# Attention and a gated MLP on one core: GpSimd's broadcasts of reciprocals go ahead of its copies of P, and one copy of P moves to ScalarE

## The chip, the cores and the metric

One core of a Trainium2 chip runs the kernel. The metric is the device time of one execution in microseconds (us). The core's engines are TensorE (PE in the profile; PEld is its weight load), VectorE (DVE), ScalarE (ACT), GpSimd (POOL) and SyncE (SP, which here only issues DMAs).

## The reference

Causal attention by blocks of 64 over batch 8, 8 heads, 576 positions and head size 64, then a gated MLP over all 4608 tokens:

```python
scores = scale * np.matmul(q, k.transpose(0, 1, 3, 2))
scores = np.where(block_i >= block_j, scores, -1e9)
attn = np.exp(scores - scores.max(-1, keepdims=True))
attn = attn / (attn.sum(-1, keepdims=True) + 1e-9)
x = np.matmul(attn, v)                    # (8, 8, 576, 64) -> (4608, 512)
gate = 1 / (1 + np.exp(-(x @ w_gate)))    # w_gate, w_val: 512 x 1536
out = (gate * (x @ w_val)) @ w_out        # w_out: 1536 x 512
```

## The kernel before

The work is done on pairs of heads: 32 pairs, four to a batch. A script written out by hand (FRONT) runs the first pairs, up to some 125 us. Then one step of a loop over p runs for each pair until some 460 us, and in the same stretch TensorE multiplies the first third of the MLP's hidden units (L179, L188) for the batches that are done; those matmuls are dealt between the attention's at a set rate, about 36 of them in a step. After that the rest of the MLP runs with TensorE busy throughout (L1341, L1411).

In a step, the table REST sets the order in which parts are issued, and so how each engine's queue stands, for the pair p and the two ahead of it. Three pairs are in work at once:

- **"AV"** and **"fin"** of pair p-2: TensorE multiplies the turned probabilities in the tile G by V (L358, `bank<-G,VS`, 44 matmuls), and VectorE multiplies the result by the broadcast reciprocals `rb` (L703, `xT<-bank,rb`), which also frees the PSUM bank pair that AV wrote. There are three such bank pairs. The scores of pair p take two of them right behind AV and need the third, AV's own, for their last block. ScalarE then makes the high part of xT (L831) and GpSimd the low part (L844, "xl").
- **"s"**, **"t"** of pair p: scores on TensorE (L358, with KH, KL, QH, QL), maxima on VectorE (L487, L541), eight exps on ScalarE (L499) and a ninth for the last 64 positions (L543), all into a buffer Z or XB by turns.
- **"tr3"**, **"tr2"**, **"trm"** of pair p: VectorE turns the exps in place by 32x32 blocks (L598, three instructions; the last, of 1408 columns, waits for L543). Behind it come the sums plus 1e-9 (L565), the reciprocal (L566) and a turned copy `rT` (L568), and GpSimd's queue writes rT to DRAM (`r_d<-rT`).
- **"mv"** and **"mc"** of pair p-1: the turned blocks are moved between groups of 32 partitions into G, in 16 quarters of 32x800. Nine go by DMA (L621, four from GpSimd's queue and five from SyncE's), three are copied by ScalarE (L624) and four by GpSimd (L615, `move_pool`). G has one buffer, so this starts when AV of the pair ahead is done.
- **"rb"** of pair p-1: three DMAs from GpSimd's queue (L292, `rb<-r_d`) read the reciprocals from DRAM and broadcast them over 64 partitions each.
- **"k"**, **"ql"**, **"q"**: K and Q of pair p+1 are turned (L390) and split in high and low parts: KH on ScalarE (L395), KL on GpSimd (L405), QL on VectorE (L409).

Everything on one engine is executed in its queue's order. ScalarE's third copy, of quarter (2, 2), stands behind the exp of the sixth score block by a line in `move`; the first two come when AV has freed G. `hL` (L218) is the low part of the MLP's hidden values: on GpSimd, or on VectorE for the last of a batch's four.

Of the kernel before, what the change touches and what calls it, by code (L numbers as in the profile page):

```python
# [21 lines left out]
AHEAD = 3  # L22
KEEP = 11

REST = (("AV", 0), ("fin", 0), ("s", 3), ("mv", 0), ("xl", 0), ("mc", 0), ("rb", 0), ("t", 4), ("tr3", 1), ("tr2", 1), ("k", 0), ("trm", 0), ("ql", 0), ("q", 0), ("trl", 1), ("trt", 2))
NB = 25
B_OF = {2: (0, 3), 3: (6, 4), 0: (14, 1), 1: (16, 2)}
LT = 14
# [45 lines left out]
def attn_glu_kernel(ctx: ExitStack, tc: tile.TileContext, q, k, v, w_gate, w_val, w_out, out):  # L74
# [26 lines left out]
    def behind(ins, other):  # L101

        tc.add_manual_dep(ins, other.name, mybir.DependencyInfo(mybir.DependencyClass.NoSync,
                                                                mybir.DependencyReason.DATA), reason="order")
# [123 lines left out]
    with ExitStack() as s2:  # L228
# [105 lines left out]
        maxima, exps = [], []  # L334
# [3 lines left out]
        def mark(engine, ins):  # L338
            last[engine] = ins.ins

        def chain(engine, ins):
            if not scripted and engine in last:
                behind(ins.ins, last[engine])
            mark(engine, ins)
# [83 lines left out]
        def attend(p):  # L428
# [179 lines left out]
            def quarter(k):  # L608
                c, a = k if isinstance(k, tuple) else quarters[k]
                return dict(out=Gc[32 * c:32 * c + 32, a], in_=Zc[32 * a:32 * a + 32, c])  # L610

            def move_pool():

                for k in (8, 10, 11, (3, 3)):
                    chain("POOL", nc.gpsimd.tensor_copy(**quarter(k)))  # L615

            def move():

                for k in range(12):
                    if k not in (8, 10, 11):  # L620
                        ins = (nc.sync if k % 2 else nc.gpsimd).dma_start(**quarter(k))  # L621
                        (mark if k % 2 else chain)("moves" if k % 2 else "POOL", ins)
                for i in range(3):
                    ins = nc.scalar.copy(**quarter((i, i)))  # L624
                    if i > 1:
                        behind(ins.ins, exps[-3])
                    mark("ACT", ins)

            def tr_main(i):
# [219 lines left out]
            def step(what, is_fine=False, alt=False, queue=nc.sync):  # L849
# [4 lines left out]
                elif what[0] == "s":  # L854
                    s_blocks({"s3": (3,), "s2": (2,), "sl": (1, 0)}[what])
                elif what == "t":
                    s_tail()
                elif what == "rb":
                    if moved:
                        recip(2, nc.gpsimd)  # L860
                elif what == "trm":
                    if moved:
                        turned()
                    else:
                        recip()
                elif what == "mv":
                    if moved:
                        move()
                elif what == "mc":
                    if moved:  # L870
                        move_pool()
                elif what == "xl":
                    lower_x()
                elif what in ("tr3", "tr2"):
                    tr_main(int(what[2]))
                elif what == "trl":
                    tr_low()
                elif what == "trt":
                    tr_tail()
                elif what == "fin":  # L880
                    finish()
                else:
                    av()
# [388 lines left out]
        for p in range(N_FIRST + 1, n + 1):  # L1272
# [5 lines left out]
            tick = 0  # L1278
            for what, places in REST:
                if what == "AV" and far:  # L1280
# [24 lines left out]
                for _ in range(places if now else 6 if what == "tr3" else 0):  # L1305
                    pe_ticks.append(pe_last[0])
                    acc += rate
                    while acc >= 1:
                        acc -= 1
                        left -= 1  # L1310
                        ins = next(mlp, None)
# [256 lines left out]
```

## Time and profile before

| what | value |
|---|---|
| median of 3 runs | 1099.28 us (1096.95 to 1099.8) |
| the profiled execution | 1099.69 us |
| its span, first to last instruction | 1097.8 us |
| TensorE busy | 1080.7 us (98%) |
| VectorE busy | 862.1 us (79%) |
| ScalarE busy | 602.7 us (55%) |
| GpSimd busy | 532.3 us (48%) |
| granted TensorE clock | 1.000 of 2.4 GHz |

The span is what the profiler saw of the core; the execution's time is 1.89 us longer. Busy shares are means over stages that differ: the engines other than TensorE are full in the stage of the loop and half idle in the MLP that follows.

### The profile page before, as it was taken

The numbers are of one execution on the slowest core, as the hardware profiler recorded it, in microseconds if no ns is written. First come the engines' busy times: TensorE is split into PE (matmuls) and PEld (weight loads), VectorE is DVE, ScalarE is ACT, GpSimd is POOL, SyncE is SP. The second block draws the span as 40 slices with busy tenths as digits, with TensorE's granted clock in tenths as the row PEclk, the third lists the DMA queues.
The fourth block names the chain that finished last, engine by engine and source line by source line (L and its number), as shares of the span: only waits on it lengthen the run. The fifth ranks groups of instructions, "written<-read, shape, count | busy, mean of one in ns | idle before, by whom it ended". The sixth has DMA issues, their size and how long they took to land.

```text
span 1097.8 us, 19466 instructions
## 1 busy us (share of the span) xinstructions
PE 1080.7 (98%) x6593; PEld 929.5 (85%) x6593; DVE 862.1 (79%) x1488; ACT 602.7 (55%) x1321; POOL 532.3 (48%) x692
## 2 busy tenths in 40 slices
PE   8899999999999999999999999999999999999998
PEld 6577777778787778778899999999999999999997
DVE  6899999898989898787699768578785585665744
ACT  6887777777787777643353444534454142341421
POOL 3655499898989898710113030321305336243340
PEclk9999999999999999999999999999999999999999
DMA  8797599899888887745033362350886517345251
GB/s 162 162 206 159 128 184 190 187 189 197 185 194 177 200 175 184 198 122 170 22 97 103 123 221 78 144 187 34 293 296 230 188 50 224 103 128 186 74 164 58
DMA packets 264619, 174.87 MB, mean 159 GB/s; under 512 B 200988, under 2 KB 222092, under 8 KB 263880
## 3 DMA queue, kind: packets, MB, share of 16 engines
q1 hardware_dynamic: 247000, 148.54, 50.6%
q0 software_dynamic: 7008, 17.68, 6.9%
q10 hardware_dynamic: 10512, 7.41, 2.3%
q8 instruction: 52, 0.85, 0.3%
q14 instruction: 47, 0.39, 0.1%
HBM read 104.73 MB, written 47.60 MB: 139 GB/s over the span
## 4 chain that ended last, share of the span: by engine, by line
PE 83%; DVE 4%; DMA 4%; ACT 3%; POOL 2%; issue 2%; SPq 1%; ACTq 0%; DVEq 0%; POOLq 0%
PE b L1341 32%; PE m L1411 12%; PE bank L358 11%; PE m L179 10%; PE m L188 7%; PE b L1411 7%; PE bank L179 3%; SPq L292 1%; DMA rqk<-in_q_dram 1%; DMA rqk<-in_k_dram 1%; DMA rb<-r_d 1%; PE bank L188 1%; POOL G L615 1%; PE bank L363 1%; ACT XB L499 1%
## 5 line engine op out<-in xcount | busy, mean ns | idle before, releaser
L1341 PE MATMUL b<-XH,w 128*128 128x384 f32 x1344 | 349.0, 335 | 0.0
L1341 PEld LDWEIGHTS b<-XH,w 128*128 128x128 f32 x1344 | 243.8, 188 | 3.6
L1341 PE MATMUL b<-XL,w 128*128 128x384 f32 x672 | 223.5, 335 | 0.0
L1136 POOL TENSOR_TENSOR XB<-XB 128x384 f32<-128x384 f32 x20 | 21.5, 1076 | 238.0 <-DMA XB<-xT_d 238.0
L1341 PEld LDWEIGHTS b<-XL,w 128*128 128x128 f32 x672 | 126.1, 188 | 1.7
L1411 PE MATMUL m<-wo,hH 128*128 128x512 f32 x368 | 119.9, 391 | 0.0
L358 PE MATMUL bank<-G,VS 128*64 128x64 f32 (+3 forms) x1264 | 95.0, 305 | 2.6 <-POOL G L615 1.5
L358 PEld LDWEIGHTS bank<-G,VS 128*64 128x64 f32 x1264 | 64.6, 137 | 35.1 <-issue 7.6
L1364 ACT ACTIVATE g<-g 128x384 f32<-128x384 f32 x72 | 37.8, 525 | 93.1 <-DVE g L1377 49.3
L1149 ACT CAST XH<-XB 128x1536 fp32r<-128x1536 f32 (+2 forms) x72 | 65.1, 941 | 35.7 <-DVE XB L1147 27.3
L188 PE MATMUL m<-wo,hH 128*128 128x512 f32 x256 | 83.8, 393 | 0.0
L179 PE MATMUL m<-XH,wg 128*128 128x512 f32 x240 | 81.2, 394 | 0.4 <-ACT t L203 0.4
L179 PE MATMUL m<-XH,wv 128*128 128x512 f32 x240 | 81.2, 395 | 0.0
L1411 PEld LDWEIGHTS m<-wo,hH 128*128 128x128 f32 x368 | 69.0, 188 | 12.9
L487 DVE TENSOR_REDUCE nm<-bank 128x2 f32<-128x1024 f32 (+1 forms) x96 | 76.9, 801 | 2.2 <-ACT Z L499 0.6
L1150 DVE TENSOR_TENSOR XL<-XB,XH 128x1536 fp32r<-128x1536 f32 (+2 forms) x72 | 75.8, 1085 | 0.0
L1411 PE MATMUL m<-wo,hL 128*128 128x512 f32 x184 | 72.1, 392 | 0.0
L1411 PE MATMUL b<-wo,hH 128*128 128x512 f32 (+1 forms) x216 | 71.4, 383 | 0.0
L1405 POOL TENSOR_TENSOR pr<-pr,pr 128x512 f32<-128x512 f32 x33 | 42.6, 1296 | 42.6 <-DMA pr<-part_d 29.6
L499 ACT ACTIVATE Z<-bank,nm 128x512 f32<-128x512 f32 (+3 forms) x104 | 53.5, 529 | 7.8 <-DVE nm L487 4.5
L188 PEld LDWEIGHTS m<-wo,hH 128*128 128x128 f32 x256 | 47.9, 188 | 9.9 <-issue 0.2
L1349 POOL TENSOR_TENSOR hL<-v,hH 128x384 fp32r<-128x384 f32 x36 | 38.9, 1094 | 33.0 <-ACT hH L1348 30.3
(219 smaller groups left out, 2626.3 us busy)
## 6 DMA issues: line engine op xcount, KB each, us to landing
pr<-part_d SPq DMA_DIRECT2D x66, 256.0 KB
XB<-xT_d SPq DMA_DIRECT2D x16, 576.0 KB
part_d<-pr SPq DMA_DIRECT2D x36, 256.0 KB
rqk<-in_q_dram SPq DMA_DIRECT2D x120, 72.0 KB
rqk<-in_k_dram SPq DMA_DIRECT2D x120, 72.0 KB
out_dram<-pr SPq DMA_DIRECT2D x33, 256.0 KB
wgv_d<-st SPq DMA_DIRECT2D x8, 896.0 KB
w<-wgv_d SPq DMA_DIRECT2D x4, 1792.0 KB
```

What stands on the lines that cost most here:

```text
L179: mm = nc.tensor.matmul(ps, lhsT=lh, rhs=rh, start=(i == 0), stop=(i == n - 1))
L188: mm = nc.tensor.matmul(ps, lhsT=lh[:, f, t * P:(t + 1) * P], rhs=rh, start=(f == i == 0), stop=(f == F1 - 1 and i == 2))
L358: pe_last[:] = [pin("PE", nc.tensor.matmul(*args, **kw)).ins]
L487: mark("DVE", nc.vector.tensor_reduce(out=nm_()[:, c0:c0 + 2], in_=ps[:, :, c:c + n], axis=AX.X, op=ALU.max, negate=True))
L499: mark("ACT", nc.scalar.activation(out=dst, in_=src, func=AF.Exp, bias=nm_()[:, c0 + h:c0 + h + 1], accum_out=sm[:, 5 * h + i:5 * h + i + 1]))
L1149: nc.scalar.copy(out=XO[j][0][:, a:b], in_=x)
L1150: sub = nc.vector.tensor_sub(out=XO[j][1][:, a:b], in0=x, in1=XO[j][0][:, a:b].bitcast(F32))
L1341: mm = nc.tensor.matmul(ps, lhsT=lh, rhs=rh, start=(first and k == 0), stop=(k == n - 1), skip_group_check=not first)
L1349: (nc.vector if q else nc.gpsimd).tensor_sub(out=hL[:, f, n:n + N2], in0=h, in1=hH[:, f, n:n + N2].bitcast(F32))
L1364: mark2("ACT", nc.scalar.activation(out=t, in_=c, func=AF.Tanh, scale=0.5))
L1405: nc.gpsimd.tensor_add(out=pr[t], in0=pr[t], in1=other)
L1411: mm = nc.tensor.matmul(po[t][:, cols], lhsT=lh[:, f, t * P:(t + 1) * P], rhs=wo[:, f, e, cols], start=((whole or half == 0) and i == 0), ...
```

## The change

In REST, "rb" stands ahead of "mc", so GpSimd issues the three broadcasts ahead of its copies. GpSimd copies three quarters, not four, and ScalarE copies the fourth, quarter (3, 3), behind the exp of the eighth score block.

```diff
-REST = (... ("mv", 0), ("xl", 0), ("mc", 0), ("rb", 0), ("t", 4), ...)
+REST = (... ("mv", 0), ("xl", 0), ("rb", 0), ("mc", 0), ("t", 4), ...)
...
             def move_pool():
 
-                for k in (8, 10, 11, (3, 3)):
+                for k in (8, 10, 11):
                     chain("POOL", nc.gpsimd.tensor_copy(**quarter(k)))
...
-                for i in range(3):
+                for i in range(4):
                     ins = nc.scalar.copy(**quarter((i, i)))
                     if i > 1:
-                        behind(ins.ins, exps[-3])
+                        behind(ins.ins, exps[-3 if i == 2 else -1])
                     mark("ACT", ins)
```

GpSimd's queue in one step of the loop (L621 are its four moves, L844 the low part of xT, L218 and L402 belong to the MLP and to the next pair's Q):

```order
 L621 DMA G<-XB 32x800 x4
 L844 TENSOR_TENSOR XL_435<-xT,XH_434 128x576
-L615 COPY G<-XB 32x800 x4
-L292 DMA rb<-r_d 64x576
-L292 DMA rb<-r_d 64x64
-L292 DMA rb<-r_d 64x512
+L292 DMA rb<-r_d 64x576
+L292 DMA rb<-r_d 64x64
+L292 DMA rb<-r_d 64x512
+L615 COPY G<-XB 32x800 x3
 L218 TENSOR_TENSOR hL<-h_1925,hH 128x512
 L402 TENSOR_SCALAR KQ<-KQ 128x128
```

The three broadcasts have moved ahead of the copies, and one copy is gone.

ScalarE's queue in the same step (the exps of one pair, the last two of the eight and the ninth):

```order
 L214 CAST hH<-h_1925 128x512
 L499 ACTIVATE Z,sm_108<-bank,nm 128x4x32 x2
+L624 COPY G<-XB 32x800
 L543 ACTIVATE Z,sm_108<-bank,nm 128x4x160
 L203 ACTIVATE t<-m 128x512
```

The new copy stands between the eighth exp and the ninth. It stands there in every step of the loop that has the moves, 22 of 23; in the last one four copies follow each other.

VectorE's queue once, near the end of the loop (L703 is xT of the last pair but one, L1062 to L1140 prepare weights and sums for the second part of the MLP):

```order
 L1062 TENSOR_SCALAR raw<-cT 128x512
+L1064 SCALAR_TENSOR_TENSOR raw<-raw 128x512
+L1065 TENSOR_TENSOR cT<-cT,raw 128x512
 L703 TENSOR_TENSOR xT<-bank,rb 128x320
 L703 TENSOR_TENSOR xT<-bank,rb 128x256
 L1136 TENSOR_TENSOR XB<-XB 128x384
-L1064 SCALAR_TENSOR_TENSOR raw<-raw 128x512
+L1095 TENSOR_TENSOR cT<-cT 128x128
 L1139 TENSOR_TENSOR XB<-XB 128x384
 L1140 TENSOR_TENSOR XB<-XB 128x384
-L1065 TENSOR_TENSOR cT<-cT,raw 128x512
```

Two instructions of the weights' preparation have moved ahead of that pair's xT.

## Rows read from the trace of the kernel before

**Rows 1.** Windows: busy us (instructions) of PE, PEld, DVE, ACT, POOL; clock, DMA, GB/s.
```profile
150.00:450.00 300.00, 295.51 (x2242) 234.52 (x2242) 266.29 (x445) 231.44 (x567) 272.23 (x412) 1.00 0.88 189
```

**Rows 2.** Waits of PE, 130 to 470 us: total us, times, longest.
```profile
PE bank L358 <- DVE xT L703: 2.1, 5, 0.8
PE bank L358 <- POOL G L615: 1.5, 1, 1.5
```

**Rows 3.** Chain that ended last, loop: start us, us, what.
```profile
228.53 4.34 PE bank L358 x56
...
242.99 4.89 PE bank L358 x66
...
257.11 4.89 PE bank L358 x66
...
271.24 4.34 PE bank L358 x56
...
285.68 4.34 PE bank L358 x56
...
328.41 3.81 PE bank L358 x50
...
343.26 4.89 PE bank L358 x66
```

**Rows 4.** Timeline of POOL from 265 us: start us, us, engine, line, instruction.
```profile
265.77 3.54 POOL L615 COPY G<-XB 32x800 f32<-32x800 f32 x4
269.26 1.57 POOL L292 DMA_DIRECT2D rb<-r_d  x3
...
271.42 1.40 POOL L405 TENSOR_TENSOR KL<-KQ,KH 128x576 fp32r<-128x576 f32 x1
```

**Rows 5.** Timeline of DVE from 260 us, in brackets idle time before.
```profile
260.06 0.82 DVE L703 TENSOR_TENSOR xT<-bank,rb 128x320 f32<-128x320 f32 x2 [0.92 <-PE bank L358]
...
271.40 0.13 DVE L565 TENSOR_SCALAR sm<-sm 128x9 f32<-128x9 f32 x1
...
274.62 0.82 DVE L703 TENSOR_TENSOR xT<-bank,rb 128x320 f32<-128x320 f32 x2 [1.32 <-DMA rb<-r_d]
```

**Rows 6.** Source line L624, loop: duration ns min/median/max.
```profile
L624 ACT COPY G<-Z x36: 856/860/862, 130.8 to 446.7; 32x800 f32<-32x800 f32 x36
```

**Rows 7.** Timeline of ACT, pair whose AV starts at 228.46 us.
```profile
225.94 0.79 ACT L543 ACTIVATE XB<-bank,nm 128x640 f32<-128x640 f32 x1
...
227.18 0.69 ACT L395 CAST KH<-KQ 128x576 fp32r<-128x576 f32 x1
```

**Rows 8.** Timeline of DVE, the same pair.
```profile
227.01 1.60 DVE L598 STREAM_TRANSPOSE XB<-XB 128x1408 f32<-128x1408 f32 x1
...
228.54 0.51 DVE L565 TENSOR_SCALAR sm<-sm 128x9 f32<-128x9 f32 x1
...
231.97 0.81 DVE L703 TENSOR_TENSOR xT<-bank,rb 128x320 f32<-128x320 f32 x2
```

**Rows 9.** Timeline of POOL, the same pair.
```profile
227.74 1.28 POOL L218 TENSOR_TENSOR hL<-h,hH 128x512 fp32r<-128x512 f32 x1
```

**Rows 10.** Source line L409, 195 to 430 us: duration ns min/median/max.
```profile
L409 DVE SCALAR_TENSOR_TENSOR QL<-KQ,QH x16: 581/770/1476, 201.4 to 416.6; 128x448 fp32r<-128x448 f32 x16
```

**Rows 11.** Timeline of POOL at 431 us.
```profile
431.51 0.78 POOL L292 DMA_DIRECT2D r_d<-rT  x1 [1.29 <-DVE rT L568]
```

**Rows 12.** Timeline of DVE at the end of the loop.
```profile
461.69 0.82 DVE L703 TENSOR_TENSOR xT<-bank,rb 128x320 f32<-128x320 f32 x2
...
462.88 0.69 DVE L1064 SCALAR_TENSOR_TENSOR raw<-raw 128x512 f32<-128x512 uint32 x1
```

**Rows 13.** Timeline of PE there.
```profile
466.28 1.83 PE L358 MATMUL bank<-G,VS 128*64 128x320 f32 x12 [0.45 <-ACT G L465]
```

**Rows 14.** Tile rb, loop: durations of its issues on POOL, ns.
```profile
L292 POOL DMA_DIRECT2D rb<-r_d x69: 516/524/541, 141.2 to 454.2; - x69
```

**Rows 15.** DMA issues by line, loop: count, KB each, median us to landing.
```profile
r_d<-rT POOLq DMA_DIRECT2D x23, 16.0 KB, 3.4
```

More of the change, by code (lines that the diff above doesn't have):

```diff
@@ L23 @@
 KEEP = 11
-REST = (("AV", 0), ("fin", 0), ("s", 3), ("mv", 0), ("xl", 0), ("mc", 0), ("rb", 0), ("t", 4), ("tr3", 1), ("tr2", 1), ("k", 0), ("trm", 0), ("ql", 0), ("q", 0), ("trl", 1), ("trt", 2))
+REST = (("AV", 0), ("fin", 0), ("s", 3), ("mv", 0), ("xl", 0), ("rb", 0), ("mc", 0), ("t", 4), ("tr3", 1), ("tr2", 1), ("k", 0), ("trm", 0), ("ql", 0), ("q", 0), ("trl", 1), ("trt", 2))
 NB = 25
```

## The prediction

> **What bounds the kernel now.** I read the windows first. In the loop over pairs TensorE is busy 295.5 of 300 us [rows 1]: what TensorE idles there, 4.5 us, and short stalls that the row counts as busy (below) are all that a change of order can give back. GpSimd (272 of 300) and VectorE (266) are nearly as full, ScalarE (231) less so. So no engine has much room, and a queue that runs late reaches TensorE soon.
>
> Next I read who ends TensorE's waits: VectorE's xT five times, 2.1 us, at most 0.8, and once GpSimd's copies into G, 1.5 us [rows 2]. The chain shows what a late xT costs even where no wait is listed. A step takes 14.12 or 14.13 us where the matmuls behind AV stand as one piece of 66 (242.99 to 257.11, 257.11 to 271.24), but 14.46 in the step at 228.53 and 14.44 at 271.24, where they break after 56: the last score block waits for AV's bank, which xT frees [rows 3]. In the step at 328.41 the break costs 14.85 - 14.12 = 0.73.
>
> The steps of a batch differ, so I number them by where they stand: 1 at 257.11, 2 at 271.24 (and 328.41), 3 at 228.53, 4 at 242.99. Step 1's xT is ready early: VectorE idles 0.92 until AV ends. Step 2's waits 1.32 for the broadcast [rows 5]. Step 3's starts without any idle time at 231.97, 3.5 us after its AV began [rows 8]: VectorE itself is late there. Step 4 loses nothing in its period.
>
> **The broadcasts earlier.** They stood behind copies from 265.77 and began at 269.26 [rows 4]; now they begin 3.5 us earlier. Step 2's wait of 1.32 for them is covered. Three issues (1.57) then stand ahead of three copies instead of behind four. A copy takes 3.54 / 4 = 0.885, so the last ends 1.57 - 0.885 = 0.7 later, counted from the start of the group, and the whole group ends 0.9 sooner. In step 2 the copies ended at 269.31, and AV began at about 271.2: 1.9 us of cover.
>
> **ScalarE's fourth copy.** 0.86 us [rows 6], 22 times directly ahead of the ninth exp. In step 3 that exp ends at 226.73 [rows 7] (its accumulator is read in the next 0.1 or so) and the long transpose begins at 227.01 [rows 8]. So 0.2 at most is slack, and the transpose begins at about 227.7 and ends at 229.3. Behind it stands L565, sums plus 1e-9, which takes 0.13 us in one place [rows 5] and 0.51 in step 3 [rows 8]. There it ended at 229.05, just as GpSimd's hL did (227.74 + 1.28 = 229.02) [rows 9]: it waited for GpSimd's instruction. The same holds for QL (L409), 0.58 to 1.48 us [rows 10]. After the change GpSimd comes to KL sooner but must wait for KH, which ends at 227.87 [rows 7] plus 0.86: KL, 1.40 long [rows 4], then runs from 228.8 to 230.2, L565 ends at 230.3, and QL no longer meets KL and takes 0.58 instead of 1.48. From L565's end to xT it was 231.97 - 229.05 = 2.92; less 0.9 that is 2.02, and xT starts at 232.35, 0.4 later. TensorE waits for just that xT, so step 3 loses **0.4** more. In the two later batches step 3 had a late step 2 ahead of it, which gave VectorE time (343.26 shows 66 in one piece [rows 3]); I take 0.3 and 0.2 there. Step 3 in four batches: **+1.3**.
>
> In step 2 the delay meets L565 too. It took 0.13 because it came at 271.40, 0.02 ahead of KL at 271.42 [rows 4, 5]. With the transpose some 0.3 later it comes while KL runs, until 272.8. It loses up to 1.4, as much as the idle 1.32 ahead of xT. So the regular step 2 trades a wait for the broadcast for one for GpSimd: bounds -0.3 and +0.3, taken **0** (the two are nearly equal). The two late ones (328.41 and its like in the next batch, 0.7 each) come down to a regular step 2's 0.3: **-0.8**. The longest single wait, 0.8 [rows 2], was for a broadcast that came late and goes: **-0.8**. Step 1 has 0.92 of cover [rows 5] for 0.86: nothing, and 0.86 in each batch if that cover were gone. The broadcasts' receivers, VS and K loads on SyncE's queue are not moved: nothing.
>
> **The first and last pairs.** Before 190 us, steps bound by VectorE lose by ScalarE's copy and gain by the broadcast; bounds -0.5 and +1.0, taken 0. At 441.94 TensorE waits 1.5 for GpSimd's copies alone [rows 2], since there AV follows its moves within one step. On GpSimd's way to them it waited 1.29 for rT [rows 11], which comes from the ninth exp: later by up to 0.86. The copies end 0.7 later for their place behind the broadcasts: 0.7 to 1.56, taken **+1.5**, since a queue that already waits for rT passes on all of it. Near 462 xT of the last pair but one is put behind L1064 (0.69 [rows 12]) and L1065, which I take alike: 1.4 us. xT began with no idle time then. ScalarE's high part of xT stands ahead of copies into G for the last pair, and TensorE waits for those already, 0.45 at 466.28 [rows 13]. Bounds 0 and 1.4; I take **+0.9**, since the matmuls of two other banks come in between.
>
> **The sum.** 1.3 - 0.8 - 0.8 + 1.5 + 0.9 = **+2.1 us**. The profiled execution took 1099.69 us (span 1097.8 and 1.89 around it): 1101.8. It stands 0.41 over the median of the runs, 1099.28, so the median should be **1101.4**, 0.2% slower. A difference under 0.3%, 3.3 us, is about what a measurement cannot tell from none.
>
> **A rule that speaks against it.** Rows first: GpSimd's issue of a broadcast took 516 to 541 ns in all 69 cases [rows 14], those under VectorE's transposes too (269.26 to 270.83 [rows 4] lies across one). The Trainium skill, "SBUF — State Buffer", section "SBUF: two separate sides", says that GpSimd cannot write the descriptors of its DMAs while VectorE runs an instruction in a mode that takes both ports. If transposes were of that kind, three issues put under two of them would each be held. By the row that costs nothing; by the rule the copies behind would come later, which is rival C.
>
> **Rivals.**
>
> A, *ScalarE's 0.86 passes whole* (ends slower). Steps 2 and 3 are the ones where VectorE has no room; if L598's delay there reaches xT undiminished, because QL still meets KL, eight steps lose 0.86 each, 6.9, in place of the +1.3 and the -0.8 above: 6.9 - 0.8 + 1.5 + 0.9 = 8.5, less the 2.0 of step 2's stalls for the broadcast that go: +6.5, **1105.8**. For it: no idle time ahead of step 3's xT. Against: QL's 0.9. It decides from 0.25 us of delay in step 2.
>
> B, *VectorE gets free of GpSimd* (ends faster). GpSimd is 0.9 shorter in each step. If L565 and QL then meet neither hL nor KL, step 3 (0.34 in four, less what the late ones lack, about 0.7 in all), step 2 (0.3, 0.3, 0.7, 0.7) and the 0.8 go: -3.5, and at the end of the loop the 1.5 shrinks to 0.7 and the 0.9 to 0. That is -2.8, and with the waits before 190 us (0.5 to 1 more) -3.5: **1095.8**. For it: L565 has taken 0.13. Against: KL must wait for KH now.
>
> C, *the issues are held*. Up to 1.6 for a transpose, so in step 2 copies end 0.7 + 0.86 + 1.6 = 3.2 later against 1.9 of cover: 1.3 in four steps: 1101.4 + 5.2 = **1106.6**. Against it: the 69 equal issues.
>
> D, *the broadcasts don't come earlier*, since they wait for r_d to land, 3.4 us after its issue [rows 15]. That issue ends long before GpSimd's moves, of which four and the low part of xT lie in between; only a write that takes over 5 us would hold them, and then also the copies behind. Price: without the 0.8 twice, 1101.4 + 1.6 = **1103.0**.
>
> **How the numbers follow.** Forecast 0.55 (its own range 1098.5 to 1103.5), A 0.22, B 0.13, C 0.04, D 0.06. Of 1098.5 to 1103.5 a small part is over the 0.3% bound (1102.6), some 0.05, and half of D: slower 0.22 + 0.04 + 0.05 + 0.03 = 0.34. Faster is B but for a part under the bound: 0.11. Same is the rest, 0.55. The range, 1095.5 to 1106.0, reaches to A and B and leaves out C.
>
> **What would show it.** The broadcasts issued right behind XL, 3.5 us sooner, and no wait of xT for them: right for the first step. The ninth exp and the long transpose 0.86 and some 0.7 later against AV, L565 ending with KL, and step 3's period at 14.8 to 14.9: right for the second. TensorE's wait for the copies near 442 near 3 us, and xT near 462 behind L1065. The prediction is wrong if step 3's period is 14.5 or less (then B), if step 2's goes over 14.7 (then A or C), or if VectorE's xT still waits for rb (then D).

## The result, and the profile after

The change makes the kernel slower: median 1106.49 us (1104.76 to 1108.83, six runs) against 1099.49 (six runs of before beside them), a ratio of 1.0063 with a 95% interval of 1.004 to 1.0087. The prediction was 1101.4, slower too, but within what can't be told from no change; 1106.49 lies outside its range, which ended at 1106.0. The profiled execution has a span of 1105.7 us, 7.9 more than before, and a mean granted clock of 0.996 of 2.4 GHz. The one run of the six whose mean clock was 1.000 took 1104.76, so the clock alone does not make the loss.

First, who ends TensorE's waits, as in [rows 2] (130 to 480 us; total us, times, longest):

```profile
PE bank L358 <- POOL G L615: 3.0, 1, 3.0
PE bank L358 <- ACT G L465: 2.4, 1, 2.4
PE bank L358 <- DVE QL L409: 1.4, 2, 0.7
```

The waits for VectorE's xT are gone, but the single wait for GpSimd's copies has doubled, and one for ScalarE's copies at the end has grown from 0.45 [rows 13] to 2.4. The second table of waits is VectorE's, 130 to 430 us, after:

```profile
DVE XB L598 <- ACT XB L543: 8.6, 11, 0.9
DVE Z L598 <- ACT Z L543: 7.2, 10, 1.5
```

and the rows of before that these replace:

```profile
DVE xT L703 <- DMA rb<-r_d: 6.0, 4, 2.7
...
DVE Z L598 <- ACT Z L543: 0.4, 1, 0.4
DVE XB L598 <- ACT XB L543: 0.2, 1, 0.2
```

In this stretch VectorE no longer waits for a broadcast ahead of xT; it waits for the ninth exp ahead of the long transpose instead, 21 times, 15.8 us. One wait has taken the place of another.

The windows show what no table of waits shows (4 us each: busy us of PE, PEld, DVE, ACT, POOL, then TensorE's granted clock):

```profile
444.00:448.00 4.00, 3.18 (x36) 2.45 (x38) 3.58 (x5) 1.17 (x4) 3.07 (x4) 0.72 0.76 230
448.00:452.00 4.00, 4.00 (x26) 2.97 (x23) 1.42 (x3) 2.46 (x3) 2.60 (x6) 0.85 0.36 81
472.00:476.00 4.00, 3.47 (x13) 1.58 (x14) 0.69 (x1) 0.65 (x2) 0.00 (x0) 0.63 0.92 160
```

The clock is 1.00 in this whole stretch of before; after, it falls to its lower level, 1.2 GHz, for 3.41 us behind each of the two long waits (from 445.77 and from 473.08). The timeline of TensorE has the AV groups that stand in these windows, with the idle time ahead of each in brackets:

```profile
125.70 2.93 PE L358 MATMUL bank<-G,VS 128*64 128x320 f32 x28
...
431.01 2.97 PE L358 MATMUL bank<-G,VS 128*64 128x256 f32 x44
...
444.82 4.62 PE L358 MATMUL bank<-G,VS 128*64 128x256 f32 x44 [3.01 <-POOL G L615]
...
460.82 2.97 PE L358 MATMUL bank<-G,VS 128*64 128x256 f32 x44
...
472.53 2.98 PE L358 MATMUL bank<-G,VS 128*64 128x320 f32 x12 [2.40 <-ACT G L465]
...
478.18 1.31 PE L358 MATMUL bank<-G,VS 128*64 128x64 f32 x16
```

and the same of before:

```profile
126.95 2.28 PE L358 MATMUL bank<-G,VS 128*64 128x320 f32 x20
...
429.65 2.97 PE L358 MATMUL bank<-G,VS 128*64 128x256 f32 x44
441.94 2.97 PE L358 MATMUL bank<-G,VS 128*64 128x256 f32 x44 [1.49 <-POOL G L615]
456.53 2.97 PE L358 MATMUL bank<-G,VS 128*64 128x256 f32 x44
...
470.31 1.31 PE L358 MATMUL bank<-G,VS 128*64 128x64 f32 x16
```

The same 44 matmuls take 4.62 us where the clock is down, and the last pair's 12 take 2.98 for 1.83 [rows 13]. The Trainium skill, "TensorE: Matmul & The Clock Gate", "Part 1: The HAM clock gate", says that an idle TensorE drops to half its rate; the level of 1.2 GHz agrees, and the row gives the price here: 1.65 us on AV alone.

From AV of the eighth pair (126.95 before, 125.70 after) to the second part of the last AV it is 343.36 us before and 352.48 after: 9.1 more. It stands in these places, each the difference of two starts:

| stretch | before | after | more | predicted |
|---|---|---|---|---|
| first pairs, to AV at 214.03 / 213.93 | 87.08 | 88.23 | +1.15 | 0 |
| four steps 2 | 58.51 | 58.81 | +0.30 | -0.8 |
| four steps 3 | 57.18 | 58.35 | +1.17 | +1.3 |
| four steps 4 | 56.51 | 57.51 | +1.00 | 0 |
| three steps 1 | 43.42 | 42.41 | -1.01 | -0.8 |
| to the AV with the wait for GpSimd | 12.29 | 13.81 | +1.52 | +1.5 |
| from it to the next AV (clock down) | 14.59 | 16.00 | +1.41 | none |
| to the last AV | 9.75 | 11.71 | +1.96 | +0.9 |
| to its second part (clock down) | 4.03 | 5.65 | +1.62 | none |
| sum | | | +9.12 | +2.1 |

In the profiled execution of after the start, up to the eighth pair, was 1.25 us shorter, so its span grew by 7.9; the medians of the runs differ by 7.0. What follows the last AV takes the same in both. The loop in the table, its first five rows, is +2.6; the two waits at its end with what the clock adds are +6.5.

Now the chain of links, one at a time. GpSimd in the step of [rows 4]:

```profile
265.48 1.43 POOL L844 TENSOR_TENSOR XL<-xT,XH 128x576 fp32r<-128x576 f32 x1
266.86 1.57 POOL L292 DMA_DIRECT2D rb<-r_d  x3
268.48 2.64 POOL L615 COPY G<-XB 32x800 f32<-32x800 f32 x3
```

The broadcasts go out right behind XL, and no issue is held: the 69 issues take 518 to 544 ns, as before. Next ScalarE, VectorE and GpSimd around the AV at 228.52, a step 3 ([rows 7 to 9] in before):

```profile
225.68 0.86 ACT L624 COPY G<-Z 32x800 f32<-32x800 f32 x1
226.56 0.80 ACT L543 ACTIVATE XB<-bank,nm 128x640 f32<-128x640 f32 x1
```

```profile
227.48 1.65 DVE L598 STREAM_TRANSPOSE XB<-XB 128x1408 f32<-128x1408 f32 x1 [0.77 <-ACT XB L543]
229.05 0.97 DVE L565 TENSOR_SCALAR sm<-sm 128x9 f32<-128x9 f32 x1
...
230.90 0.58 DVE L409 SCALAR_TENSOR_TENSOR QL<-KQ,QH 128x448 fp32r<-128x448 f32 x1
...
232.00 0.82 DVE L703 TENSOR_TENSOR xT<-bank,rb 128x320 f32<-128x320 f32 x2
```

```profile
228.58 1.41 POOL L405 TENSOR_TENSOR KL<-KQ,KH 128x576 fp32r<-128x576 f32 x1 [0.61 <-ACT KH L395]
```

L565 starts 0.5 later and ends at 230.02, 0.03 behind GpSimd's KL; QL takes 0.58 instead of 1.48, and xT starts 3.48 behind its AV, as before (3.51).

The step still takes 0.16 more, and it loses that at its end, ahead of the next AV. ScalarE's ost (L963) and t (L203) read the PSUM bank m, into which TensorE multiplies the MLP; the last weight load ahead of AV (PEld) waits for them. After, the end of ost and that load:

```profile
241.93 0.59 ACT L963 ACTIVATE ost<-m 128x512 f32<-128x512 f32 x1
```

```profile
242.56 0.19 PEld L188 LDWEIGHTS m<-wo,hH 128*128 128x128 f32 x1 [0.20 <-ACT ost L963]
```

and before, where ost ended 0.68 ahead of the last two loads, which follow each other without a wait:

```profile
240.87 0.60 ACT L963 ACTIVATE ost<-m 128x512 f32<-128x512 f32 x1
```

```profile
242.15 0.41 PEld L188 LDWEIGHTS m<-wo,hH 128*128 128x128 f32 x2
```

After, from 199 to 431 us, TensorE starts 13 of 17 AVs 0.41 to 0.92 us behind the start of the matmul ahead, and in each of the 13 the last weight load begins 0.04 behind the end of a t or an ost. Before, all 17 stand at 0.32. Together that is 2.6 us, 0.6 of it in a step where the table of waits names a DMA of part_d (0.53). Waits as short as these do not show in the table of TensorE's waits.

Last, the end of the loop, VectorE and ScalarE ([rows 12] in before):

```profile
465.03 0.69 DVE L1064 SCALAR_TENSOR_TENSOR raw<-raw 128x512 f32<-128x512 uint32 x1
465.75 0.69 DVE L1065 TENSOR_TENSOR cT<-cT,raw 128x512 f32<-128x512 f32 x1
466.36 0.82 DVE L703 TENSOR_TENSOR xT<-bank,rb 128x320 f32<-128x320 f32 x2
...
470.66 0.68 DVE L207 SCALAR_TENSOR_TENSOR h<-t,m 128x512 f32<-128x512 f32 x1
```

```profile
469.39 0.80 ACT L465 COPY G<-bank 128x768 f32<-128x768 f32 x1 [0.30 <-PE bank L363]
471.37 0.62 ACT L214 CAST hH<-h 128x512 fp32r<-128x512 f32 x1 [1.19 <-DVE h L207]
471.90 0.75 ACT L465 COPY G<-bank 128x512 f32<-128x512 f32 x2
```

xT stands behind L1064 and L1065, as foreseen. What was not foreseen is on ScalarE: hH, which waits for VectorE's h, has come to stand ahead of the last two copies into G. In before it stood behind them.

### The profile page after: what moved, and what is told of

The parts are those of the page before. It is cut to its first block, busy times and chain, and to the rows that moved or that the text cites. A ratio compares the mean times of both kernels' runs of the same rounds, so it can differ in the third digit from the quotient of the medians.

```text
span 1105.7 us, 19473 instructions
## 1 busy us (share of the span) xinstructions
PE 1085.9 (98%) x6593; PEld 934.6 (85%) x6593; DVE 862.4 (78%) x1488; ACT 623.9 (56%) x1344; POOL 509.9 (46%) x669
## 4 chain that ended last, share of the span: by engine, by line
PE 75%; DMA 8%; DVE 6%; SPq 4%; ACT 3%; issue 2%; POOL 1%; ACTq 0%; DVEq 0%; POOLq 0%
PE b L1341 32%; PE m L1411 11%; PE bank L358 10%; PE b L1411 6%; PE m L179 6%; PE m L188 5%; PE bank L179 3%; SPq L292 3%; DMA rqk<-in_k_dram 2%; DMA VS<-in_v_dram 1%; DMA rb<-r_d 1%; ACT XB L499 1%; DVE nm L487 1%; DVE KQ L390 1%; PE bank L188 1%
## 5 line engine op out<-in xcount | busy, mean ns | idle before, releaser
L358 PE MATMUL bank<-G,VS 128*64 128x64 f32 (+3 forms) x1264 | 98.0, 310 | 7.8 <-POOL G L615 3.0
L358 PEld LDWEIGHTS bank<-G,VS 128*64 128x64 f32 x1264 | 69.8, 140 | 37.2 <-issue 8.0
```

Source lines behind the costliest of these rows:

```text
L358: pe_last[:] = [pin("PE", nc.tensor.matmul(*args, **kw)).ins]
```

## The experiments

Theory 1, formed after the comparison: the loss lies in separate places, which can be mended one by one. They are the place of GpSimd's copies at the last pair that has the moves (n - 3, the wait near 442), ScalarE's copy ahead of the ninth exp (the loop), and VectorE's order at the end. Theory 2 is in each expectation the rival to that. A *loop* below is the time from AV of the eighth pair to the AV at 429.65 in before, where it takes 302.70 (305.31 after). It is read from one execution of each kernel. Up to there e5_only_last and e8_fill_before are the program of before, and took 301.50 and 302.82; e3_last_old and e6_end are that of after, and took 305.78 and 305.45. So differences of some 1 us are between executions, and after's loss, about 3 us, is not.

**e1_order**: the kernel before, with the new order in REST alone.

```diff
-... ("xl", 0), ("mc", 0), ("rb", 0), ("t", 4), ...
+... ("xl", 0), ("rb", 0), ("mc", 0), ("t", 4), ...
```

> The order alone: GpSimd issues the broadcasts ahead of its copies and still makes four; ScalarE makes three. Theory 1 (the loss has three parts: ScalarE's copy ahead of the ninth exp makes VectorE late in the loop; near 445 us GpSimd's copies come so late that TensorE waits 3.0 us and then runs at the half clock; near 472 us xT behind two other VectorE instructions gives a second such wait): no VectorE delay, xT's waits for rb gone (up to -3 us), GpSimd's copies end 1.57 later, so TensorE waits about 3.06 near 442 and the clock falls once (+1.6 and +1.65), VectorE's order at the end is the old one. Sum about 0: 1098 to 1101. Theory 2 (ScalarE's copy is the whole loss, wherever it stands): -2 to -3, 1096.5 to 1097.5. Theory 3 (the order is the loss): over 1104.

1101.16, ratio 1.0026 (1.0017 to 1.0035), just over the expected range. Loop 302.35: step 2 came down to 14.13, and step 3 went up to 14.82 to 14.95. What the earlier broadcast gives in one step VectorE lacks in the next. The wait near 441 is 3.04, for GpSimd's copies, and the clock falls behind it (AV 4.62); the end is as before.

**e2_copy**: the changed kernel with the old order in REST, so only the shift of one copy from GpSimd to ScalarE.

> The copy alone: ScalarE makes four copies and GpSimd three, broadcasts behind the copies as before. Theory 1: VectorE late by ScalarE's 0.86 in steps 2 and 3, near 442 the copies end 0.9 sooner for their number and 0.8 later for rT, so TensorE waits 1.4 and the clock stays up; xT near 462 is not behind the two instructions. 1100.5 to 1102.5. Theory 2: about all of the loss, 1105 to 1107. Theory 3: 1099, as before.

1103.84, 1.0053 (1.0041 to 1.0065), more than expected. Loop 305.10, nearly the whole of after's loss in the loop. The wait near 441 is 2.54. The last copies of ScalarE and GpSimd had ended at 442.75 and 442.80, 1.1 ahead of AV, so it is not shown what ended it. In the profiled execution the clock did not fall there:

```profile
443.89 2.97 PE L358 MATMUL bank<-G,VS 128*64 128x256 f32 x44 [2.54 <-ACT Z L543]
```

At the end xT of the last pair but one stands ahead of L1064, as in before, but hH stands ahead of the last two copies into G, as in after:

```profile
469.31 0.62 ACT L214 CAST hH<-h 128x512 fp32r<-128x512 f32 x1 [0.35 <-DVE h L207]
469.84 0.75 ACT L465 COPY G<-bank 128x512 f32<-128x512 f32 x2
```

TensorE waits 1.56 for them, and the stretch to the last AV takes 10.87 us for 9.75.

**e3_last_old**: the changed kernel, but pair n - 3 with the old order and four copies on GpSimd.

```diff
-for k in (8, 10, 11):
+for k in (8, 10, 11, (3, 3)) if p == len(pairs) - 3 else (8, 10, 11):
...
-att[p - 1](what)
+att[p - 1]({"mc": "rb", "rb": "mc"}.get(what, what) if p - 1 == n - 3 else what)
```

> The change, but for the pair whose AV follows its moves within one step (near 442 us) the old order and the old share of copies. Theory 1: the wait there is 1.5 + 0.8 = 2.3 and not 3.0; 0.7 us less, and if the clock then stays up 1.65 more: 1104 to 1106, with the second wait near 470 still there. Theory 2: as the change, 1106.5.

1107.45, 1.0075 (1.0063 to 1.0088): no gain. The wait is still 2.9, 1.4 more than in before, and GpSimd's queue is late ahead of it: it issues r_d 2.76 us behind the AV at 430.76, where it was 1.86 in before (431.51 [rows 11] behind 429.65). That is 0.9 of the 1.4; the rest is not shown.

**e6_end**: the changed kernel, with L1064 put behind xT of the last pair but one.

```diff
-nc.vector.scalar_tensor_tensor(out=Ef, in0=lo, scalar=2.0 ** -52, in1=Ef, ...)
+low = nc.vector.scalar_tensor_tensor(out=Ef, in0=lo, scalar=2.0 ** -52, in1=Ef, ...)
+if first:
+    behind(low.ins, first)
...
-sums_gv(*early[0], alone=last["DVE"])
+sums_gv(*early[0], alone=last["DVE"], first=divided[n - 2])
```

> The change, with xT of the last pair but one held ahead of L1064 in VectorE's queue near 470 us. Theory 1: TensorE's wait of 2.4 there falls to under 1 and the half clock behind it goes: 1.5 to 2 and 1.6 less, 1102.5 to 1103.5. Theory 2: as the change, 1106.5; the wait there has another cause.

1103.17, 1.0039 (1.0027 to 1.0051): the end is back at 9.75 and 4.03, without a fall of the clock, 3.3 us under after. hH stands behind the copies into G again, too:

```profile
468.26 1.53 ACT L465 COPY G<-bank 128x768 f32<-128x768 f32 x3 [0.62 <-PE bank L363]
470.36 0.62 ACT L214 CAST hH<-h 128x512 fp32r<-128x512 f32 x1 [0.57 <-DVE h L207]
```

**e4_late**: e6_end, with ScalarE's fourth copy behind the ninth exp, ahead of KH.

```diff
-... ("t", 4), ("tr3", 1), ...
+... ("t", 4), ("ma", 0), ("tr3", 1), ...
...
-                for i in range(4):
+                for i in range(3 if late else 4):
...
+                elif what == "ma":
+                    copy_self(3)
```

> The change with xT near 470 us held ahead of L1064 (as in e6_end, 1103.2), and ScalarE's fourth copy behind the ninth exp, ahead of KH, instead of ahead of it. Theory 1 (the copy costs because the ninth exp, and VectorE's long transpose and reciprocals behind it, come 0.86 later): the loop from the first pair with moves to the AV near 430 takes 302.7 to 303.2 us again, not 305.4; rT is 0.8 earlier near 432, so TensorE's wait for the copies near 442 is 2.2 and the clock may stay up. 1099 to 1101. Theory 2 (ScalarE's copy costs wherever it stands, now over KH, KL and QL): 1102.5 to 1104.

1099.18, 1.0007 (0.9993 to 1.002): as before. Loop 302.31; VectorE's waits for L543 are two again, 0.4 and 0.3. TensorE's waits for t and ost ahead of AV are still there, 2.7 us in the loop.

The wait near 441 is 2.38, and here the clock fell behind it (AV 4.53).

**e5_only_last**: the kernel before, with the new order at pair n - 3 alone (the line on att of e3_last_old).

> The kernel before, with the broadcasts ahead of the four copies for one pair alone, the one whose AV follows its moves within a step (near 442 us). Theory 1 (the half clock follows TensorE's long wait): the wait grows from 1.49 to 3.06, the AV behind it takes 4.6 and not 2.97, granted clock 0.5 for 3.4 us, the loop ahead and the end as before: +2.9 to +3.2, about 1101.5. Theory 2 (the clock falls for another reason, such as the changed loop): the wait alone, +1.5.

1100.95, 1.0016 (1.0001 to 1.003). The wait is 3.04, AV takes 4.62, and the two periods there grow by 1.56 and 1.43: one exchange in one step costs 3.0 in the trace, half of it by the wait, half by the clock.

**e7_fill** is e1_order, **e8_fill_before** the kernel before, each with matmuls of the MLP taken from later places and dealt ahead of the AV that waits (13 and 7 of them).

```diff
+if p == n - 2:
+    for _ in range(7):
+        ...
+        behind(ins, hold[0])
+        behind(ins, pe_ticks[-1 - AHEAD])
+    rate -= 7 / (TICKS + 11)
```

> The order alone for all pairs (e1_order, 1101.2), with 13 of the MLP's matmuls (13 x 0.228 = 3.0 us) dealt ahead of the AV near 441 instead of behind it. Theory 1: the wait of 3.04 is filled, the clock stays up, and what the order gains in the loop is left: -3.0 -1.5 from 1101.2, so 1096.7, under the kernel before. Theory 2 (the loss of the order lies elsewhere): 1100 to 1101.

> The kernel before, with 7 of the MLP's matmuls (1.6 us) dealt ahead of the AV near 442. Theory 1: its wait of 1.49 is filled: 1097.0, and the difference to e7_fill is what the order is worth in the loop, 0.3 to 0.5. Theory 2 (a wait filled there comes back at the end of the loop): as before, 1098.4.

1105.28, 1.0056 (1.0035 to 1.0076), and 1104.33, 1.0048 (1.003 to 1.0065): both expectations missed. The wait near 441 is gone, and the one for L465 at the end is 4.8 and 5.0, with the clock down for 6.83 us behind it. It is not shown that the work taken from there is what is missing: 13 and 7 matmuls give nearly the same wait, and in both kernels hH has come to stand ahead of the last three copies into G, where it waits 3.0 and 3.5 us for VectorE's h. ScalarE in e8_fill_before, and the window behind it:

```profile
467.12 0.62 ACT L214 CAST hH<-h 128x512 fp32r<-128x512 f32 x1 [3.50 <-DVE h L207]
467.64 1.45 ACT L465 COPY G<-bank 128x768 f32<-128x768 f32 x3
```

```profile
470.00:474.00 4.00, 4.00 (x14) 2.06 (x11) 0.00 (x0) 0.00 (x0) 0.00 (x0) 0.50 0.24 46
```

**e9_last**: e4_late, with pair n - 3 as before (the two edits of e3_last_old).

> The changed kernel with xT ahead of L1064 at the end and ScalarE's fourth copy behind the ninth exp (as in e4_late), and the last pair that has the moves (n - 3) done wholly as before the change: copies ahead of broadcasts, four on GpSimd and three on ScalarE. Theory 1 (three places make up the loss, and the last of them is the copies' place at pair n - 3): TensorE's wait near 441 is 1.4 to 1.6 us again, the clock stays at its upper level there, AV(29) takes 2.97, and the time is 3 us below e4_late: 1096.2, 0.2% under before. Theory 2 (what is taken from this wait comes back at the end, as it did with the fill): as e4_late, 1099.2.

1098.28, 0.9997 (0.9988 to 1.0006). The wait is 1.19, AV takes 2.97, and the mean clock was 1.000 in ten of eleven runs. The mechanism is Theory 1's; the gain that was expected beside before, 0.2%, is not there (TensorE waits 0.6 for VectorE's h in its place).

**e10_dma**: the changed kernel, but quarter (3, 3) goes by a tenth DMA, from SyncE's queue, not by ScalarE. It differs from after in this alone.

```diff
-                for i in range(4):
+                mark("moves", nc.sync.dma_start(**quarter((3, 3))))
+                for i in range(3):
                     ins = nc.scalar.copy(**quarter((i, i)))
                     if i > 1:
-                        behind(ins.ins, exps[-3 if i == 2 else -1])
+                        behind(ins.ins, exps[-3])
```

> The changed kernel, but the sixteenth quarter (3, 3) is moved by a tenth DMA, from SyncE's queue with the five that are there, and ScalarE keeps its three copies: GpSimd has the broadcasts first and three copies, ScalarE nothing more than before. Theory 1 (it is ScalarE's copy ahead of the ninth exp that costs the loop 2.5 us): the loop from AV p7 to AV(28) takes 302.3 or less, L598 no longer waits for L543, and what is left is the wait near 442 at about 2.2 (1.5 and 0.7 of a copy's place), with the clock's fall or without it: 1099 to 1101. Theory 2 (VectorE is the bound whichever engine copies, and GpSimd's order against KL and hL costs it): loop 305 as in the changed kernel, 1104 or more. A third outcome, the DMA landing later than a copy, would show as AV waiting for DMA G in each step.

1098.54, 1.0003 (0.9994 to 1.0012), a little under the expected range. Loop 299.27: from 184 us on every step takes 14.12 or 14.13. VectorE now waits for TensorE ahead of xT, in nearly each step:

```profile
DVE xT L704 <- PE bank L358: 15.2, 15, 2.4
```

Of the third outcome there is one case: the first AV behind the moves, at 143.63, waits 1.33 for a DMA into G. The two waits at the end are there still, 2.10 and 2.47, and behind the second the clock falls.

**e11_late_copy**: e4_late with the old order in REST.

> e4_late with the old place of the broadcasts (behind GpSimd's three copies): what is left of the change is the fourth copy on ScalarE, behind the ninth exp. Theory 1: the loop takes 302 to 302.7 (the broadcasts come 0.9 sooner than before, and the copy costs VectorE nothing), the wait near 441 is 0.9 shorter on GpSimd and set by ScalarE's late copy instead, about 1.5, without a fall of the clock: 1097 to 1098.5. Theory 2 (the copy costs VectorE something wherever it stands, by KH, which comes later and with it KL and L565): loop 304 or more, 1101.

1100.58, 1.0011 (0.9999 to 1.0024), over the expected range. Loop 301.85; the profiled execution took 1098.07, and its clock stayed up behind both waits:

```profile
439.30 2.97 PE L358 MATMUL bank<-G,VS 128*64 128x256 f32 x44 [2.37 <-POOL KQ L402]
...
464.51 1.84 PE L358 MATMUL bank<-G,VS 128*64 128x320 f32 x12 [1.56 <-ACT G L465]
```

Its runs fall in two groups by their mean granted clock, and so do those of other kernels with one long wait (runs and their median):

| kernel | wait near 441 | clock 1.000 | clock 0.996 to 0.998 |
|---|---|---|---|
| e1_order | 3.04 | 3 runs, 1099.82 | 8 runs, 1101.40 |
| e5_only_last | 3.04 | 4 runs, 1099.28 | 8 runs, 1101.74 |
| e4_late | 2.38 | 6 runs, 1098.32 | 5 runs, 1100.63 |
| e11_late_copy | 2.37 | 5 runs, 1098.80 | 6 runs, 1101.43 |
| before, beside e11_late_copy | 1.49 | 23 runs, 1098.39 | 2 runs, 1101.32 |

Runs at 0.999 are left out (one of e4_late, two of before); of before's runs beside the other experiments 0 of 17, 4 of 24 and 1 of 17 were at 0.998 or less. The same program has the fall in one run and not in the next. In the four experiments the runs with it are slower by 1.6 to 2.6 us; the two of before, 0.7 and 5.2 over the others, give no price. The wait is that of the one execution profiled; how long it was in the other runs is not known.

**e12_all**: e10_dma with both ends mended: pair n - 3 in the old order, L1064 behind xT as in e6_end, and hH put behind the last copy into G.

```diff
-pin("ACT", nc.scalar.copy(out=hH, in_=got[1]))
+ins = pin("ACT", nc.scalar.copy(out=hH, in_=got[1]))
+if copied:
+    behind(ins.ins, copied[-1])
```

> e10_dma (sixteenth quarter by SyncE's DMA, broadcasts first, three copies each on GpSimd and ScalarE) with the two ends mended: pair n - 3 has its copies ahead of the broadcasts, and at the end xT of the last pair but one stands ahead of L1064 and ScalarE's hH behind the last copies into G, as before the change. Theory 1 (the end's loss comes only from these two orders): the loop keeps e10_dma's 299.3, the wait near 441 is about 0.6 (1.49 less a copy's 0.88), the end is 9.75 and 4.03 again without a fall of the clock: 1094 to 1095.5, 0.3% under before. Theory 2 (time that is won in the loop comes back as a wait at the end, as the copies into G of the last pair need what ScalarE and VectorE do there however early TensorE comes): the end's wait stays over 2 us, 1097.5 to 1099.

1096.46, 0.9981 (0.9969 to 0.9993): faster than both kernels, if by less than was expected. Loop 298.79; TensorE's AV groups at the end (L362 is L358 of the others):

```profile
437.29 2.97 PE L362 MATMUL bank<-G,VS 128*64 128x256 f32 x44 [0.80 <-ACT Z L505]
...
453.30 2.97 PE L362 MATMUL bank<-G,VS 128*64 128x256 f32 x44
463.20 1.84 PE L362 MATMUL bank<-G,VS 128*64 128x320 f32 x12 [0.60 <-ACT G L469]
```

The end takes 9.90 and 4.03, with hH behind the copies. Of the 3.9 won in the loop 1.4 goes again between 437 and 453, where TensorE waits for h, which stands behind a late xT: with the old order at n - 3 that pair's broadcast lands late, as the table of waits and the chain show:

```profile
PE m L179 <- DVE h L209: 1.4, 1, 1.4
```

```profile
438.05 5.33 DMA rb<-r_d
```

## Why the prediction was wrong

**The broadcasts earlier**: right. They go out behind XL, and the waits of xT for them are gone. Rivals C and D fall with that: the issues are as long as before, and step 2 lost its wait.

**Step 3**: right in size (+1.17 for +1.3), but in part by luck. The first links hold: L565 ends with KL (230.02, predicted 230.3) and QL takes 0.58. But the loss is spread otherwise: 0.16, 0.19, 0.46 and 0.36 in the four batches for 0.4, 0.4, 0.3 and 0.2, with a period of 14.5 to 14.7 and not 14.8 to 14.9. In the first two xT starts no later behind its AV than before (3.48 and 3.49 for 3.51 and 3.50), and all of the loss stands ahead of the next AV, where TensorE waits for ScalarE's ost. In the other two xT starts 0.4 later, 0.3 and 0.2 come by the last score block, which waits for it, and the rest by ost.

**Step 2**: wrong. "The two late ones come down to a regular step 2's 0.3: -0.8" gave -0.23, and the regular ones, taken at 0, cost 0.53. The wait for xT went as foreseen: counted from AV, the last score block starts 0.1, 0.4 and 0.6 earlier in three of them; in the one at 271.49 a wait of 0.3 for QL takes its place. But each of the four loses 0.4 to 0.5 ahead of the next AV, where TensorE waits for ScalarE's t. Their period, 14.6 to 14.8, is over the 14.7 named for A or C in two of the four. Step 1's single wait went as said (-1.01 for -0.8). Step 4 cost 1.0 where nothing was expected: 0.5 of it is one wait for a DMA of part_d in one step, the rest 0.1 per step, by t again.

**The first pairs**: taken at 0, with a bound of +1.0; they cost 1.15. That is not between executions: the three of before's program took 86.2 to 87.2 us there, the three of after's 88.2 to 88.5. The first AV behind the moves, at 143.58, is 0.8 of it: TensorE waits 0.69 there, and not at all in before.

**The loop as a whole** was read too narrowly. "ScalarE's 0.86 passes whole" (A) and "VectorE gets free of GpSimd" (B) stood as rivals, each with part of the chance, but a gain of B's size and a loss of A's size are both there. Who moves quarter (3, 3) gives:

| quarter (3, 3) moved by, broadcasts first | kernel | loop |
|---|---|---|
| GpSimd | e1_order | 302.35 |
| a DMA | e10_dma | 299.27 |
| ScalarE, behind the ninth exp | e4_late | 302.31 |
| ScalarE, ahead of the ninth exp | after | 305.31 |

Without the copy on either engine the loop is 3.4 under before: B's mechanism, which had been given 3.5 in all. ScalarE's copy ahead of the ninth exp costs 6.0 from there, near A's 6.9, but not in A's way: in step 3 QL does not meet KL, and in no step 2 or 3 of the loop's four batches does xT start more than 3.5 behind its AV. Behind the ninth exp it costs 3.0, and 2.7 of that are TensorE's waits for t and ost ahead of AV. These waits are in each kernel whose ScalarE makes the fourth copy, ahead of the exp or behind it, and in none where it makes three (before, e1_order, e5_only_last, e8_fill_before, e10_dma, e12_all). The sum, +2.6, is near neither A nor B. A's 1105.8 comes close to the measured time, but by another sum: it had no term for the clock. That is luck.

**The wait near 442**: right, +1.52 for +1.5, with the listed wait at 3.01 for "near 3 us".

**The steps that failed** are two. One is ScalarE's fourth copy: it was priced only by way of the ninth exp, VectorE and xT, and the loop was put at 1.3 - 0.8 - 0.8 = -0.3. It measured +2.6, in large part since TensorE also waits for what ScalarE reads from the MLP's bank, 0.1 to 0.5 us in three steps of four, and nothing in the forecast stood for that. Mending the copy's place in e4_late took the median from 1103.17 to 1099.18.

The other is the price of the waits at the end: each was set at its own length. Behind the wait near 442 the clock fell, +1.41; the forecast had no such term. The term "+0.9, since the matmuls of two other banks come in between" measured +1.96, and the clock added 1.62. The 1.4 by which xT moves was bounded right, but hH's new place on ScalarE, behind which two copies into G waited for VectorE's h, was not looked at: the forecast followed VectorE's order there and not ScalarE's. In e6_end L1064's place was mended and hH's returned with it. The shares can be read from e2_copy and e11_late_copy, where xT is ahead of L1064 and hH ahead of the last two copies: the wait is 1.56 and the end takes 10.87 and 10.86 for 9.75. So hH's place is worth about 1.1 of the 1.96, and VectorE's order the rest. With xT ahead of L1064 and hH ahead of three copies (e7_fill) the wait was 4.77.

The clock, 3.0, and the wait at the end, 1.1 over its term, are 4.1 of the 7.0 us between 2.1 and 9.1; the steps 2 and 4 are 2.1 more and the first pairs 1.15, and steps 1 and 3 give 0.3 back.

**Open**: what decides in a run whether the clock falls (2.54 in e2_copy passed without, 2.38 in e4_late did not, each in the one execution profiled); what ends the wait near 441 where the copies into G are done earlier (e2_copy); and whether a fill for that wait pays if hH is kept behind the copies into G, as in e12_all.

## What to carry to other kernels

Rivals that work on different engines are not alternatives: price each alone, then add them, or run the version that has one without the other (here the same quarter by DMA won 6 us of the loop against ScalarE). When work moves to an engine, list all that stands behind it in that engine's queue and who waits for each, not only the chain that the edit is about: here TensorE waited for ScalarE's reads of another stage's bank, too briefly for any table of waits. Lengthening a wait of TensorE can cost nearly twice what is added, as 1.5 us here did with 1.4 by the clock's fall behind it. Where a scheduler sets the order, look at every engine's queue around the waits at the end of a stage, not only at the one whose instruction the edit moves.

## What the runs showed of the hardware

The granted clock stood at its lower level for 3.41 us behind single waits of 2.38 to 3.04 us in TensorE's queue, and for 6.83 us behind waits of 4.8 and 5.0, with TensorE 98% busy over the span; waits of 2.10, 2.37 and 2.54 passed without a fall in the executions profiled. AV of 44 matmuls took 2.97 at the upper level and 4.53 to 4.62 across a fall. In the same kernel (e11_late_copy) five runs of eleven had no fall. With the tenth DMA on SyncE's queue, 0.59 us of issue, all steps from 184 us on took 14.12 or 14.13, with the DMA engines at 0.87 of their time from 150 to 450 us; the one wait for it was 1.33 at the first AV behind the moves.
